# An attention kernel without its closing barrier, with its first two projection chunks interleaved and its last product cut unevenly

## The chip, the cores and the metric

The kernel runs on one core of a Trainium2 chip. A core has five engines, each with its own instruction stream: TensorE (PE in the profile, with its weight loads shown apart as PEld), VectorE (DVE), ScalarE (ACT), GpSimd (POOL) and SyncE (SP, which here issues every DMA). [...] The metric is device time in microseconds (us).

## The reference

Eight sequences of 112 queries are projected, attend to cached keys and values with 32 heads, and are projected back. All inputs and the output are bf16.

```python
B, Sq, D = 8, 112, 640
H, Sk, Dh = 32, 512, 192
q = transpose((x @ wq).reshape(B, Sq, H, Dh), 0, 2, 1, 3)
scores = einsum("bhqd,bhkd->bhqk", q, k_cache) * Dh ** -0.5
p = softmax(scores, axis=-1)
o = einsum("bhqk,bhkd->bhqd", p, v_cache)
return transpose(o, 0, 2, 1, 3).reshape(B, Sq, H * Dh) @ wo
```

The caches are 50 MB each and are read once.

## The kernel before

**Units.** `build_main` handles heads in `NG = 8` groups of four. A unit is one group of heads of one sequence, so there are `NU = 64` units. For each unit PE computes the scores (`do_S`, L925), ACT takes the exponential of them (L1023), PE multiplies by the values (`do_PV`, L943; a column of ones beside the values gives the row sums), DVE and ACT divide by those sums (`do_NM`: the reciprocal L1089 and the scaling L1092 on DVE; `norm` L1030 on ACT), PE transposes the result (`do_T`, L954), and ACT copies it into `oT` (L1040).

**Projections.** For each group, six chunks of 128 query columns are projected (`("Q", g, c)`), and after the attention of a group seven row tiles of 128 rows go through its part of `wo` (`("O", g, m)`), whose partial products DVE adds up in `acc` (`do_OE`, L1101 and L1104). Both kinds are called pairs, since each has two halves that go to PSUM banks 6 and 7. A table written out by hand (`slot`, filled by `put` and `halves`) gives each iteration `i` up to two of them: slot `(i, 0)` stands between the transposes and the product with the values, slot `(i, 1)` after that product. Before a pair writes a bank, `bank_free` waits until the pair before it has been copied out: for an O pair this is the semaphore `vO`, which DVE raises in `do_OE`.

**The start.** The first group is projected in two halves of the rows (`do_Q0`). For the first half of the rows, chunks 0 to 3 read `wq` as it landed, with four narrow matmuls (32 columns of weights each, L871) for each of the `DC = 5` blocks of the contraction; chunks 4 and 5 read a copy that POOL has reordered (L864). Chunk 0 waits for each of the five loads of `wq` (`mW0`) as it comes to it. Even chunks go to bank 6, odd ones to bank 7, and a chunk waits until ACT has copied out the chunk two before it (`aQ`).

**Keys.** Each unit's keys come as four loads into one of three buffers `kr`, and DVE transposes them in four instructions (`do_KT`, L1083) into `kt`. `kt_ahead` says how many of them DVE has done by each iteration; from iteration 17 on it is always the transposes 1, 2 and 3 of one unit and transpose 0 of the next. SP issues the loads in one fixed order (L1284). A load of keys waits until the fourth transpose of the unit that had its buffer is done (`vKT`), and everything behind it in SP's order waits with it.

**DVE's order in an iteration** (L1127 to L1138): up to three key transposes (`kts[:3]`), then the evacuation of the O pair in slot `(i, 0)`, then the reciprocal and scaling of unit `i - 1`, then the O pair in slot `(i, 1)`, then the remaining transposes.

**The end.** The last O pair (`apart` in `do_pair`) finishes one half of 320 columns before it starts the other. For each of the seven row tiles SP sends the 128 x 640 result to HBM when both halves have been added (L1287), and at last waits for all seven (L1290).

**Fallback and blocks.** POOL counts row sums outside a safe range; the count reaches every engine as a register (`get_flag`). `br_eq` (L1306) then sends the engines past a second, slower kernel that is only there for a count above zero, and that isn't entered here. The work of each engine is written inside one `nc.Block()` (L834; its closing instructions carry L757 in the profile). Such a block makes each engine branch into instructions of its own at the start, and at the end each engine branches out and takes part in a barrier of all five; only after it comes `br_eq`.

Of the kernel before, what the change touches and what calls it, by code (L numbers as in the profile page):

```python
# [666 lines left out]
def build_main(nc, x, k_cache, v_cache, wq, wo, out, flag, regs, hints):  # L667
    B, SQ, D = x.shape
# [7 lines left out]
    HQ = R // 2  # L676
    HO = D // 2
    scale = float(DH) ** -0.5
    LO, HI = 2.0 ** -30, 2.0 ** 40
# [77 lines left out]
    with ExitStack() as es:  # L757
# [3 lines left out]
        def sem(name):  # L761
            return es.enter_context(nc.semaphore(name))
# [48 lines left out]
        mWO = [[sem(f"mWO{j}{c}") for c in range(3)] for j in range(2)]  # L811
        mOUT = [sem(f"mOUT{j}") for j in range(MT)]
        XM = [(0, 2), (2, 4), (4, MT)]
# [19 lines left out]

        block = es.enter_context(nc.Block())  # L834

        @block.tensor
        def _(pe):
            def do_X(m):
# [8 lines left out]
            def held(out, lhsT, rhs, start, stop):  # L847
# [4 lines left out]
                    ldweights=False))  # L852

            def do_Q0(c, h):
                n = q_index[0, c, h]
                if c == 0:
                    W(pe, vX, 3 if h == 0 else 4)
                    W(pe, aX, 2 if h == 0 else 4)
                W(pe, aQ, n - 1)
                for dc in range(DC):  # L860
                    if h == 1 or c >= RAW:
                        if h == 0 and c == RAW:
                            W(pe, gW0, dc + 1)
                        mm = pe.matmul(ps[:, 6 + n % 2, 0:HQ], wq0[:, dc, 128 * c:128 * (c + 1)], xT[:, dc, HQ * h:HQ * (h + 1)],  # L864
                                       start=(dc == 0), stop=(dc == DC - 1))
                        continue
                    if c == 0:
                        W(pe, mW0[dc], 16)
                    for a in range(4):
                        w0 = DH * a + 64 * (c // 2) + c % 2  # L870
                        mm = pe.matmul(ps[32 * a:32 * a + 32, 6 + n % 2, 0:HQ], wqs[:, 0, dc, w0:w0 + 63:2],  # L871
                                       xT[:, dc, HQ * h:HQ * (h + 1)], start=(dc == 0), stop=(dc == DC - 1))
                mm.then_inc(pQ, 1)

            def do_pair(i, j):
# [15 lines left out]
                for q, hs in [(q, [h]) for h in range(2) for q in steps] if apart else [(q, range(2)) for q in steps]:  # L891
                    if k == "Q":
                        w = wqs[:, g % 2, q, 128 * c:128 * (c + 1)]
                        rhs = [xT[:, q, HQ * h:HQ * (h + 1)] for h in range(2)]
                    else:
                        if c == 0 and q % 2 == 0:
                            W(pe, mWO[g % 2][q // 2], 32 * (g // 2 + 1))
                        w = oT[:, q, 128 * c:128 * (c + 1)]
                        rhs = [wos[:, g % 2, q, HO * h:HO * (h + 1)] for h in range(2)]
                    for h in hs:  # L900
# [3 lines left out]
                        for f in range(cuts):  # L904
                            cs = slice(width * f // cuts, width * (f + 1) // cuts)
                            mm = (pe.matmul if h == hs[0] and f == 0 else held)(ps[:, 6 + h, cs], w, rhs[h][:, cs], q == 0,  # L906
                                                                               q == n - 1 and f == cuts - 1)
# [57 lines left out]
            for j in range(BRIDGE):  # L965
                (held if j else pe.matmul)(ps[:, 7, 0:128], wt[:], wt[:], True, True)
            for c in range(6):
                do_Q0(c, 0)
# [22 lines left out]

        @block.scalar
        def _(act):
            W(act, vI, 1)
# [75 lines left out]

        @block.vector
        def _(dve):
            dve.memset(wt[:], 0.0).then_inc(vW, 1)
# [21 lines left out]
            def do_OE(g, m, h):  # L1095
                n = o_index[g, m, h]
                W(dve, pO, n + 1)
                src = ps[:, 6 + h, 0:HO]
                cs = slice(HO * h, HO * (h + 1))
                if g == 0:  # L1100
                    ins = dve.tensor_copy(acc[:, m, cs], src)  # L1101
# [46 lines left out]

        @block.gpsimd
        def _(gp):  # L1150
            gp.memset(ident[:], 0.0).then_inc(gI0, 1)
# [58 lines left out]

        @block.sync
        def _(sp):
            loads = []
# [65 lines left out]
            for n, (dst, src, s, count, waits) in enumerate(loads):  # L1279
# [4 lines left out]
                sp.dma_start(dst, src).then_inc(s, 16)  # L1284
            for m in range(MT):
                W(sp, vO, 2 * (MT * (NG - 1) + m + 1))
                sp.dma_start(out.rearrange("b s d -> (b s) d")[128 * m:128 * (m + 1)], ob[:, m, :]).then_inc(mOUT[m], 16)  # L1287
            get_flag(sp)
            for m in range(MT):
                sp.wait_ge(mOUT[m], 16)  # L1290


def bass_standalone__mha_block_cached__near_ridge_kernel(
# [8 lines left out]
    with nc.sbuf_tensor("flag", [1, 1], I32) as flag:  # L1302
        regs, hints = {e: nc.alloc_register(e, "raised") for e in mybir.ALL_ENGINES}, {}
        build_main(nc, x, k_cache, v_cache, wq, wo, out, flag, regs, hints)
        for e, loc in hints.items():
            nc.engines[e].br_eq(regs[e], 0, on_true="main_end", on_false="main_again").branch_hint(loc)  # L1306
# [33 lines left out]
```

## Time and profile before

| what | value |
|---|---|
| five runs | 397.04, 399.2, 396.1, 397.09, 396.75 us; median 397.04 us |
| profiled execution | 397.61 us, of which the span (first to last instruction of the kernel) is 395.8 us; 1.8 us lie around it |
| granted TensorE clock | 1.00 of full speed over the span |
| PE matmul busy | 387.4 us, 98% of the span, 8865 matmuls |
| DVE, ACT, POOL busy | 283.7 us (72%), 251.0 us (63%), 152.9 us (39%) |
| DMA | 120.00 MB, mean 303 GB/s; the hardware queue's packets take 90.4% of the 16 engines' span |

The page gives for each engine its busy time, and in 40 equal slices of the span its busy share in tenths (9 is 90% or more). The chain of waits follows the work that ended last back to the start; each of its lines is a start, a length and what ran. A timeline line is a start, a length, the engine, the source line, the operation, output and inputs with shapes, a count, and in brackets the idle time before it and what ended that. A line of the waits view says who waited for whom, and then the total in us, how often, and the longest. A source view gives for each kind of instruction of one line its count, its durations in ns as min/median/max, and its first and last start. A `q` behind an engine's name means its instruction queue.

### The profile page before, as it was taken

The numbers are of one execution on the slowest core, as the hardware profiler recorded it, in microseconds if no ns is written. First come the engines' busy times: TensorE is split into PE (matmuls) and PEld (weight loads), VectorE is DVE, ScalarE is ACT, GpSimd is POOL, SyncE is SP. The second block draws the span as 40 slices with busy tenths as digits, with TensorE's granted clock in tenths as the row PEclk, the third lists the DMA queues.
The fourth block names the chain that finished last, engine by engine and source line by source line (L and its number), as shares of the span: only waits on it lengthen the run. The fifth ranks groups of instructions, "written<-read, shape, count | busy, mean of one in ns | idle before, by whom it ended". The sixth has DMA issues, their size and how long they took to land.

```text
span 395.8 us, 19841 instructions
## 1 busy us (share of the span) xinstructions
PE 387.4 (98%) x8865; PEld 242.4 (61%) x8262; DVE 283.7 (72%) x506; ACT 251.0 (63%) x550; POOL 152.9 (39%) x352
## 2 busy tenths in 40 slices
PE   7999999999999999999999999999999999999995
PEld 2555666666566666656566566666566666667672
DVE  1665678687786777776687676877588677789833
ACT  3767765766656765666755767566674766667661
POOL 5523444334343345235343255324354233234420
PEclk9999999999999999999999999999999999999999
DMA  8999999999999999989999999989998799989811
GB/s 274 375 369 364 329 290 359 360 340 305 354 341 331 336 289 371 313 270 312 331 311 324 295 324 322 336 275 311 308 316 276 225 301 304 349 260 305 268 39 65
DMA packets 88440, 120.00 MB, mean 303 GB/s; under 512 B 9760, under 2 KB 88352, under 8 KB 88352
## 3 DMA queue, kind: packets, MB, share of 16 engines
q1 hardware_dynamic: 88352, 118.72, 90.4%
q8 instruction: 68, 1.11, 1.2%
q14 instruction: 20, 0.16, 0.1%
HBM read 117.54 MB, written 1.15 MB: 300 GB/s over the span
## 4 chain that ended last, share of the span: by engine, by line
PE 93%; DMA 3%; DVE 2%; issue 1%; SPq 1%; DVEq 0%
PE ps L943 22%; PE ps L906 21%; PE ps L848 21%; PE ps L925 21%; PE ps L954 6%; PE ps L864 2%; DMA kr<-in_k_cache_dram 1%; DMA wqs<-in_wq_dram 1%; DVE kt L1083 1%; PE ps L871 1%; SPq L1284 1%; DVE xs L1104 0%; PE ps L844 0%; DVE acc L1104 0%; DVE rinv L1089 0%
## 5 line engine op out<-in xcount | busy, mean ns | idle before, releaser
L1083 DVE STREAM_TRANSPOSE kt<-kr 128x384 int32<-128x384 int32 x256 | 192.5, 873 | 8.7 <-DMA kr<-in_k_cache_dram 8.6
L1023 ACT ACTIVATE pT<-ps 128x448 bf16<-128x448 f32 x256 | 130.6, 559 | 84.3 <-PE ps L925 84.0
L925 PEld LDWEIGHTS ps<-qT,kt 32*128 32x128 bf16 x6144 | 77.3, 93 | 31.7 <-issue 23.4
L906 PE MATMUL ps<-wos,oT 128*128 128x320 bf16 x342 | 93.0, 298 | 1.0 <-DVE xs L1104 0.7
L943 PE MATMUL ps<-vm,pT 128*128 128x193 bf16 x768 | 91.5, 247 | 0.2
L848 PE MATMUL ps<-wos,oT 128*128 128x320 bf16 (+1 forms) x340 | 91.3, 296 | 0.1
L925 PE MATMUL ps<-qT,kt 32*128 32x112 bf16 x6144 | 88.2, 208 | 1.5 <-issue 1.3
L1200 POOL TENSOR_SCALAR bad<-rinv 112x4 f32<-112x4 f32 x64 | 14.6, 228 | 192.8 <-DVE rinv L1089 192.7
L1183 POOL COPY vm<-vs 128x1152 int32<-128x1152 int32 x64 | 73.4, 1147 | 23.5 <-issue 15.0
L943 PEld LDWEIGHTS ps<-vm,pT 128*128 128x128 bf16 x768 | 67.8, 97 | 21.2 <-ACT oT L1040 11.1
L848 PE MATMUL ps<-xT,wqs 128*128 128x448 bf16 (+2 forms) x226 | 74.1, 341 | 0.0
L906 PE MATMUL ps<-xT,wqs 128*128 128x448 bf16 (+1 forms) x210 | 73.5, 350 | 0.0
L1030 ACT ACTIVATE os<-ps,rinv 112x192 bf16<-112x192 f32 x128 | 47.9, 436 | 28.3 <-DVE rinv L1089 28.3
L943 PE MATMUL ps<-vs,pT 128*128 128x193 bf16 x256 | 62.6, 245 | 0.0
L906 PEld LDWEIGHTS ps<-wos,oT 128*128 128x128 bf16 x342 | 33.2, 97 | 44.5 <-issue 37.0
L1007 ACT ACTIVATE qT<-ps 128x448 bf16<-128x448 f32 x96 | 48.0, 552 | 19.3 <-PE ps L906 12.4
L1089 DVE RECIPROCAL rinv<-ps 112x4 f32<-112x4 f32 x64 | 11.6, 182 | 58.3 <-PE ps L943 58.3
L1104 DVE TENSOR_TENSOR acc<-ps,acc 128x320 f32<-128x320 f32 x84 | 37.2, 485 | 20.7 <-PE ps L906 20.7
L1040 ACT ACTIVATE oT<-ps 128x672 bf16<-128x672 bf16 x64 | 46.4, 725 | 2.1 <-PE ps L954 2.1
L906 PEld LDWEIGHTS ps<-xT,wqs 128*128 128x128 bf16 x210 | 20.4, 97 | 34.2 <-issue 29.4
L1092 DVE TENSOR_TENSOR os<-ps,rinv 112x384 bf16<-112x384 f32 x64 | 35.7, 558 | 6.9 <-DVE rinv L1089 0.5
L1176 POOL COPY wqs<-wqr 128x384 bf16<-128x384 bf16 x70 | 33.3, 508 | 4.0 <-DMA wqr<-in_wq_dram 3.9
(42 smaller groups left out, 154.8 us busy)
## 6 DMA issues: line engine op xcount, KB each, us to landing
kr<-in_k_cache_dram SPq DMA_DIRECT2D x256, 192.0 KB, 4.1
vs<-in_v_cache_dram SPq DMA_DIRECT2D x256, 192.0 KB, 4.0
wos<-in_wo_dram SPq DMA_DIRECT2D x48, 160.0 KB, 4.2
wqr<-in_wq_dram SPq DMA_DIRECT2D x35, 192.0 KB, 5.4
out_dram<-xs SPq DMA_DIRECT2D x7, 160.0 KB, 1.8
wqs<-in_wq_dram SPq DMA_DIRECT2D x5, 192.0 KB, 4.4
xs<-in_x_dram SPq DMA_DIRECT2D x2, 320.0 KB, 3.4
xs<-in_x_dram SPq DMA_DIRECT2D x1, 480.0 KB, 5.5
```

Of the source, the lines that this page charges most:

```text
L848: return pe.add_instruction(mybir.InstMatmult(name=nc.get_next_instruction_name(), engine=mybir.EngineType.PE, ins=[pe.lower_ap_or_imm(rhs ...
L906: mm = (pe.matmul if h == hs[0] and f == 0 else held)(ps[:, 6 + h, cs], w, rhs[h][:, cs], q == 0, q == n - 1 and f == cuts - 1)
L925: mm = pe.matmul(ps[:, a, SQ * t:SQ * (t + 1)], kt[u % NT][p, t, c // 2, :, c % 2], qT[g % 2][p, c, SQ * b:SQ * (b + 1)], start=(c == 0), ...
L943: mm = pe.matmul(pv[:, k, e, 0:DH + 1], pT[u % 2][:, a, t, :], src[:, a, v0:v0 + DH + 1], start=(t == 0), stop=(t == 3), skip_group_check= ...
L1007: act.activation(qT[g % 2][:, c, HQ * h:HQ * (h + 1)], ps[:, 6 + (n % 2 if g == 0 else h), 0:HQ], ACTF.Copy).then_inc(aQ, 1)
L1023: act.activation(pT[u % 2][:, a, :, 0:SQ], ps[:, a, 0:4 * SQ].rearrange("p (t q) -> p t q", t=4), ACTF.Exp, scale=scale).then_inc(aEX, 1)
L1030: ins = act.activation(os_[u % 2][:, DH * (2 + e):DH * (3 + e)], pv_of(u)[0:SQ, 1, e, 0:DH], ACTF.Copy, scale=rinv[:, u % 4, 2 + e:3 + e])
L1040: act.activation(oT[:, :, SQ * b:SQ * (b + 1)].rearrange("p (k c) q -> p k c q", k=2), src.rearrange("p k (c q) -> p k c q", c=3), ACTF.Co ...
L1083: dve.transpose(dst, src).then_inc(vKT, 1)
L1092: dve.tensor_tensor(os_[u % 2][:, 0:2 * DH].rearrange("p (e d) -> p e d", e=2), pv[0:SQ, 0, :, 0:DH], rinv[:, u % 4, 0:2][:, :, None].broa ...
L1104: ins = dve.tensor_tensor(ob[:, m, cs] if g == NG - 1 else acc[:, m, cs], src, acc[:, m, cs], op=ALU.add)
L1183: gp.tensor_copy(vm[u % NM][:].rearrange("p a (t w) -> p a t w", w=RW)[:, :, :, 0:DH].bitcast(I32), vs[u % NV][:, :, 32:32 + 3 * DH].rearr ...
```

## The change

Five edits are made.

1. The five engine programs become plain functions that are called one after the other in the main program, so there is no block. The barrier moves into the fallback, which begins with one.
2. `do_Q0_first` replaces `do_Q0` for chunks 0 and 1 of the first half of the rows. It goes over the five contraction blocks outermost: it waits for one load of `wq`, and does the four matmuls of chunk 0 and the four of chunk 1 for it. Its matmuls are the same 40 in another order. It waits for the loads only, and chunks 2 to 5 follow as before.
3. The last O pair is cut into 384 and 256 columns (`HL`), on PE and in DVE's additions.
4. The last row tile is sent in two DMAs, the first when its first half is added.
5. On DVE, the third key transpose of an iteration moves behind the evacuation of the O pair in slot `(i, 0)`, and so stands between it and the reciprocal of unit `i - 1`. In iterations without an O pair there, nothing moves.

```diff
+    HL = 384
...
-        mOUT = [sem(f"mOUT{j}") for j in range(MT)]
+        mOUT = [sem(f"mOUT{j}") for j in range(MT + 1)]
...
-        block = es.enter_context(nc.Block())
-
-        @block.tensor
-        def _(pe):
+        def on_tensor(pe):
...
+            def do_Q0_first():
+                W(pe, vX, 3)
+                W(pe, aX, 2)
+                for dc in range(DC):
+                    W(pe, mW0[dc], 16)
+                    for c in range(2):
+                        for a in range(4):
+                            w0 = DH * a + 64 * (c // 2) + c % 2
+                            mm = pe.matmul(ps[32 * a:32 * a + 32, 6 + c, 0:HQ], wqs[:, 0, dc, w0:w0 + 63:2],
+                                           xT[:, dc, 0:HQ], start=(dc == 0), stop=(dc == DC - 1))
+                        if dc == DC - 1:
+                            mm.then_inc(pQ, 1)
...
-                        rhs = [wos[:, g % 2, q, HO * h:HO * (h + 1)] for h in range(2)]
+                        rhs = [wos[:, g % 2, q, HL * h:HL + (D - HL) * h] if apart else wos[:, g % 2, q, HO * h:HO * (h + 1)]
+                               for h in range(2)]
...
-                            cs = slice(width * f // cuts, width * (f + 1) // cuts)
+                            cs = slice(0, (HL, D - HL)[h]) if apart else slice(width * f // cuts, width * (f + 1) // cuts)
...
-            for c in range(6):
+            do_Q0_first()
+            for c in range(2, 6):
                 do_Q0(c, 0)
...
-                src = ps[:, 6 + h, 0:HO]
                 cs = slice(HO * h, HO * (h + 1))
+                if (g, m) == (NG - 1, MT - 1):
+                    cs = slice(HL * h, HL + (D - HL) * h)
+                src = ps[:, 6 + h, 0:cs.stop - cs.start]
...
-                for it in kts[:3]:
+                for it in kts[:2]:
                     do_KT(*it)
                 if i < NU:
                     do_OEs(i, 0)
+                for it in kts[2:3]:
+                    do_KT(*it)
                 if i >= 1:
                     do_NM(i - 1)
...
-            for m in range(MT):
-                W(sp, vO, 2 * (MT * (NG - 1) + m + 1))
-                sp.dma_start(out.rearrange("b s d -> (b s) d")[128 * m:128 * (m + 1)], ob[:, m, :]).then_inc(mOUT[m], 16)
+            parts = [(m, 0, D) for m in range(MT - 1)] + [(MT - 1, 0, HL), (MT - 1, HL, D)]
+            for n, (m, d0, d1) in enumerate(parts):
+                W(sp, vO, 2 * (MT * (NG - 1) + m + 1) - (d1 == HL))
+                sp.dma_start(out.rearrange("b s d -> (b s) d")[128 * m:128 * (m + 1), d0:d1], ob[:, m, d0:d1]).then_inc(mOUT[n], 16)
             get_flag(sp)
-            for m in range(MT):
-                sp.wait_ge(mOUT[m], 16)
+            for n in range(len(parts)):
+                sp.wait_ge(mOUT[n], 16)
+
+        for part, eng in ((on_tensor, nc.tensor), (on_scalar, nc.scalar), (on_vector, nc.vector), (on_gpsimd, nc.gpsimd), (on_sync, nc.sync)):
+            part(eng)
...
         with nc.body("main_again"):
+            nc.all_engine_barrier()
             build_mha_kernel(nc, x, k_cache, v_cache, wq, wo, out)
```

More of the change, by code (lines that the diff above doesn't have):

```diff
@@ L856, in do_Q0 @@
                 if c == 0:
-                    W(pe, vX, 3 if h == 0 else 4)
-                    W(pe, aX, 2 if h == 0 else 4)
+                    W(pe, vX, 4)
+                    W(pe, aX, 4)
                 W(pe, aQ, n - 1)
@@ L866, in do_Q0 @@
                         continue
-                    if c == 0:
-                        W(pe, mW0[dc], 16)
                     for a in range(4):
@@ L990, in _, with on_scalar @@
             get_flag(pe)
-        @block.scalar
-        def _(act):
+        def on_scalar(act):
             W(act, vI, 1)
@@ L1069, in _, with on_vector @@
             get_flag(act)
-        @block.vector
-        def _(dve):
+        def on_vector(dve):
             dve.memset(wt[:], 0.0).then_inc(vW, 1)
@@ L1147, in _, with on_gpsimd @@
             get_flag(dve)
-        @block.gpsimd
-        def _(gp):
+        def on_gpsimd(gp):
             gp.memset(ident[:], 0.0).then_inc(gI0, 1)
@@ L1209, in _, with on_sync @@
             get_flag(gp)
-        @block.sync
-        def _(sp):
+        def on_sync(sp):
             loads = []
```

## The prediction

> **What bounds the kernel now.** I read the page first, then the chain of waits in order of time, then the timeline at the places where that chain leaves PE, and last the source views of the closing lines.
>
> ```profile
> span 395.8 us, 19841 instructions
> PE 387.4 (98%) x8865; PEld 242.4 (61%) x8262; DVE 283.7 (72%) x506; ACT 251.0 (63%) x550; POOL 152.9 (39%) x352
> PE   7999999999999999999999999999999999999995
> ...
> DMA  8999999999999999989999999989998799989811
> ```
>
> PE is busy in every slice but the first and the last. A change inside the span therefore gains only where PE stands still, at the start, at the end, or at one of the few gaps between, and the chain of waits names these:
>
> ```profile
> 3.67 4.50 DMA wqs<-in_wq_dram
> 8.21 3.21 PE ps L871 x64
> ...
> 96.99 2.35 DVE kt L1083 x3
> 99.36 5.88 DMA kr<-in_k_cache_dram
> ...
> 106.69 0.85 DVE kt L1083
> 107.53 0.73 DVE acc L1104 x2
> ...
> 392.24 0.49 DVE xs L1104
> ```
>
> The chain starts with the last load of `wq`, which PE awaits until 8.21. Around 107 us it goes through DVE, in the only stretch of the interior where another engine's work is on it for long. It leaves PE at 392.24 for the last addition. The timeline at the first two places:
>
> ```profile
> 8.64 0.54 ACT L1007 ACTIVATE qT<-ps 128x448 bf16<-128x448 f32 x1 [2.60 <-PE ps L871]
> 9.58 0.54 ACT L1007 ACTIVATE qT<-ps 128x448 bf16<-128x448 f32 x1 [0.40 <-PE ps L871]
> ...
> 105.26 2.27 DVE L1083 STREAM_TRANSPOSE kt<-kr 128x384 int32<-128x384 int32 x3 [0.22 <-DMA kr<-in_k_cache_dram]
> 107.39 0.86 DVE L1104 TENSOR_TENSOR acc<-ps,acc 128x320 f32<-128x320 f32 x2
> 107.91 0.31 PE L906 MATMUL ps<-wos,oT 128*128 128x320 bf16 x1 [0.36 <-DVE acc L1104]
> 108.30 0.30 PE L848 MATMUL ps<-wos,oT 128*128 128x320 bf16 x1
> ```
>
> At the end, the source views of the closing lines:
>
> ```profile
> L1290 SPq EVENT_SEMAPHORE  x3: 28/28/28, 393.7 to 394.6; - x3
> L757 SPq COMPARE_BRANCH  x1: 78/78/78, 394.6 to 394.6; - x1
> L757 SPq DRAIN  x1: 7/7/7, 395.0 to 395.0; - x1
> L757 SPq EVENT_SEMAPHORE  x1: 17/17/17, 395.2 to 395.2; - x1
> L1306 SPq COMPARE_BRANCH  x1: 65/65/65, 395.3 to 395.3; - x1
> L1306 PEldq COMPARE_BRANCH  x1: 485/485/485, 395.3 to 395.3; - x1
> ```
>
> SP has seen the last output land at 394.6. Everything after it, up to 395.8, is the way out: SP's branch, the barrier, and the five branches of L1306, PE's being the longest.
>
> **The change part by part.** The sum is made against the profiled execution, 397.61 us (395.8 of span and 1.8 around it), which lies 0.57 above the median of the five runs, 397.04. I take the saving off the median.
>
> *Closing barrier.* SP's output wait ends at 394.6 and a branch of 65 to 78 ns follows it, after which SP is out; so the span would end at 394.7 in place of 395.8, a saving of 1.1. PE, ACT, POOL and DVE have their registers before 392.9 and branch out while SP still waits, so PE's 485 ns is covered by the output DMA. If SP's own branch should cost what PE's does, 0.4 of it comes back: 0.7 at least. Upward, the four engines may also do early some of what lies in the 1.8 us around the span; no row divides these, so 1.1 to 2.0. I take 1.1, the row itself.
>
> [...]
>
> *Opening branch.* SP's first DMA issue starts at 0.74, and the trace's records have its release from the opening barrier end at 0.68. The branch between is worth 0 to 0.06; I take 0.03.
>
> *First two chunks.* The loads come some 0.5 us apart (PE restarts at 6.73, 7.23, 7.69, 8.21), and four narrow matmuls start every 0.19 (3.21 us over 16 such fours with their tail), so eight fit between two loads. After 8.21 PE has 12 fours left of L871 and not 16, which would be 0.75. But chunk 2 needs bank 6, and ACT's copy of chunk 0 still runs 8.64 to 9.18, since chunk 0 still ends with the last load. PE then waits from about 8.6 to 9.24 (0.055 us is what PE takes to follow a semaphore elsewhere in this trace). Chunk 2 started at 9.36 before. The gain is 0.12; chunk 1's copy ends at 9.72, before chunk 3 needs it at 10.2. POOL's copies, which chunk 4 needs, end at 10.39, and chunk 4 moves to about 11.25. Some of it can be lost to ACT's copies later: 0 to 0.12, taken as 0.1.
>
> *Third key transpose behind the O evacuation.* At 105.26 three transposes run 0.71 apart, and only then the additions that PE awaits, though the products were done at 106.1 and 106.2. With two ahead, the additions start at 106.68 and not 107.39. Their first `vO` comes at 107.14; PE is ready for it at 107.39, the end of the product with the values. The second comes at 107.53, where PE wants it at 107.53. Two gaps go, 0.52 and 0.25 as starts stand against the usual spacing; with some 0.1 left, 0.6 is gained. Without the 0.22 us wait for keys it would still be 0.55, so it isn't an accident of one late load. The bounds are 0 (an execution where the keys come earlier) and 0.77. What is late next is the transpose itself. Who waits for it:
>
> ```profile
> SPq L1284 <- DVE kt L1083: 40.6, 89, 1.7
> ...
> DVE acc L1104 <- PE ps L906: 20.7, 28, 1.4
> DVE acc L1101 <- PE ps L906: 5.2, 5, 1.3
> ```
>
> SP queues key loads behind it, and behind these the loads of values and weights. In the iterations where DVE now idles up to 1.4 us ahead of the evacuation, the transpose comes up to 1.4 + 0.9 + 0.6 = 2.9 us later. Once it has run, the reciprocal waits for it too: at 42.50 to 43.98 DVE adds for 0.89 and idles 0.59 before the reciprocal, and a transpose of 0.72 pushes it by 0.15. PE needs that result about 1.0 us after it is ready in nearly all units (the starts of L954 against the ends of L1030 and L1092), so this push costs nothing. For the loads: DVE waits for keys 8.6 us in all, 8.1 of them in two waits before 22 us, and key transposes are some two units ahead of PE. I take nothing for it, and keep the loss as a rival.
>
> *Last product and last DMA.* PE's 12 matmuls have the same columns in all. The first half ends 0.16 later and the second at the same time, near 392.2. The last addition shrinks from 320 to 256 columns: with 482 ns for 320 and 558 ns for the 384 of L1092, about 0.41, so 0.08 earlier. The first DMA (SP issue 0.33) starts near 392.2, so SP is free for the second at 392.65. That one carries 64 KB in place of 160, and a 160 KB output lands 1.8 us after its issue, whose packets fill the last 0.5 or so. So 0.05 to 0.35; taken 0.15.
>
> [...]
>
> Sum: 1.1 + 0.03 + 0.1 + 0.6 + 0.15 = 1.98. The profiled execution would go to 395.6 and the median to **395.0 us**, 0.5% less. A measurement of this kernel can tell about 0.5% (2 us) from no change, which puts the bound at 395.05, right at the forecast.
>
> **The rivals.**
>
> *Less is had.* The gap at 107 us closes differently in other executions, or part of the barrier's 1.1 comes back after the span. Without the 0.6 the time is 395.6; with only 0.7 at the end as well, 396.0. For it: the DMA slices stand at 9, so loads in that stretch land when the queue lets them. Against: 0.55 of the gap does not need the late load.
>
> *More is had outside the span.* Four engines leave 1 to 3 us before SP. If half of the 1.8 us around the span can be done by them meanwhile, 0.9 more is gained: 394.1. For it: after the span the trace still has instruction fetches, at 396.3 to 397.8. Against: SP's own share stays.
>
> *Slower: key loads starve.* The later transpose frees a key buffer late, SP's order stands still, and with DMA at 9 tenths the lost load time can't be made up. At worst each of some 12 iterations where DVE waited over a microsecond for the O product costs one transpose of 0.72 on PE's path: 8.6 lost against 1.4 gained elsewhere, 404.2. It decides once five of them do: 3.6 - 1.4 is 2.2 us more than before. For it: SP already awaits DVE 89 times. Against: DVE waits for keys four times in all.
>
> *The change doesn't do what it says* holds for the first chunks alone: 0.1 and not 0.75 is that rival's price, already taken.
>
> **How the numbers follow.** The forecast's case has 50%, with a range of its own from 394.5 to 395.5, a little over half of it below 395.05. Less is had: 24%, within 0.5%. More: 20%, faster. Slower: 6%. So faster 0.48, same 0.46, slower 0.06. PE also stops inside its scores for up to 0.7 us at a few places that the profile calls issue (33.6 and 281.6 us), 2.4 us over the span with the smaller ones; these may fall otherwise, by 0.7 either way. The range reaches from 393.9 (the case with more, and a little beyond) to 396.6 (the smallest terms with such stops added).
>
> **What would show it.** The closing: no L757 rows, SP's branch of L1306 within 0.2 us of its last output wait, and PE's some 2 us ahead of it. The first chunks: PE idle near 0.6 us before chunk 2, and the first scores at 14.1 where they stood at 14.19. The order: no wait of L906 on DVE near 107, and PE ahead by 0.7 from there on. The end: two output DMAs for the last tile, about 0.5 us apart. The prediction is wrong if PE's busy share falls in the interior, if DVE's waits for key loads grow beyond 10 us, or if the time around the span grows by what the span loses.

## The result, and the profile after

The changed kernel took 397.14 us (median of 36 runs, 395.53 to 400.73) beside 397.68 us for the kernel before, measured with it (62 runs). The ratio is 0.9989, with a 95% interval of 0.9976 to 1.0003: by the ratio 0.44 us less (the medians differ by 0.54), and not told apart from no change. The prediction was 395.0, 1.98 us below the 397.04 it started from.

The profiled execution took 396.12 us, 394.4 of them span. First the head of the page:

```profile
span 394.4 us, 19831 instructions
PE 386.6 (98%) x8865; PEld 243.0 (62%) x8262; DVE 284.2 (72%) x506; ACT 250.8 (64%) x550; POOL 152.7 (39%) x352
```

By the span alone 1.4 us seem to be won, but nearly all of that is luck. The places that the edits touch give 0.71 at 107 us and 0.07 in the last product, and lose 0.32 at the start and 0.36 at the end: together 0.1 us. The rest comes mostly where PE stood still in the execution before at two of the stops that the prediction names (33.6 and 281.6 us), which don't come in this one. The waits view puts PE's waits ahead of scores that the profile calls issue at 1.3 us before and at 0.3 here. Single executions of one kernel differ by a microsecond and more, so what follows is read locally.

The timeline of PE at the start (L860 are the first two chunks, L880 chunks 2 and 3, L875 chunks 4 and 5):

```profile
8.09 1.12 PE L860 MATMUL ps<-xT,wqs 128*32 128x448 bf16 x20
9.67 2.08 PE L880 MATMUL ps<-xT,wqs 128*32 128x448 bf16 x40 [0.46 <-ACT qT L1017]
11.68 0.55 PE L875 MATMUL ps<-xT,oT 128*128 128x448 bf16 x2
```

PE idles 0.46 us ahead of chunk 2, for ACT's copy of chunk 0, as predicted (near 0.6 was expected). But nothing is gained here: the first scores start at 14.52, where 14.1 was predicted and 14.19 stood before. The experiments come back to that. Around 107 us, DVE and then PE:

```profile
105.28 1.58 DVE L1092 STREAM_TRANSPOSE kt<-kr 128x384 int32<-128x384 int32 x2 [0.19 <-DMA kr<-in_k_cache_dram]
106.70 0.87 DVE L1115 TENSOR_TENSOR acc<-ps,acc 128x320 f32<-128x320 f32 x2
107.50 0.83 DVE L1092 STREAM_TRANSPOSE kt<-kr 128x384 int32<-128x384 int32 x1
107.30 0.30 PE L916 MATMUL ps<-wos,oT 128*128 128x320 bf16 x1
107.62 0.30 PE L846 MATMUL ps<-wos,oT 128*128 128x320 bf16 x1
```

The additions start at 106.70 and PE has no bracket with DVE any more. Of the two gaps, 0.52 and 0.25 us over the usual spacing, 0.19 is left.

The end, from the chain of waits and the source views of the closing lines (L1302 SP's waits for the outputs, L1321 the branches):

```profile
388.68 1.80 PE ps L916 x12
390.50 0.42 DVE xs L1115
```

```profile
L1302 SPq EVENT_SEMAPHORE  x4: 17/28/28, 391.9 to 394.2; - x4
L1321 ACTq COMPARE_BRANCH  x1: 68/68/68, 389.5 to 389.5; - x1
L1321 PEldq COMPARE_BRANCH  x1: 1005/1005/1005, 389.6 to 389.6; - x1
L1321 POOLq COMPARE_BRANCH  x1: 65/65/65, 389.6 to 389.6; - x1
L1321 DVEq COMPARE_BRANCH  x1: 84/84/84, 391.1 to 391.1; - x1
L1321 SPq COMPARE_BRANCH  x1: 70/70/70, 394.3 to 394.3; - x1
```

No barrier is left, and SP branches 0.07 us after its last wait, as predicted. But that wait ends at 394.2, and the last addition at 390.93. Before, 1.82 us lay between the two (392.74 and 394.56); now it is 3.3. From the last addition to the end of the span it was 3.08 us before, and is 3.44 now. In this execution the closing has become longer, with the barrier removed and the last DMA cut.

The view of the DMA between 391.0 and 395.5, in 40 slices of 0.11 us (busy share of the 16 engines in tenths, then GB/s), shows what happened:

```profile
DMA  0039840599020000001001000000000000000030
GB/s 0 0 109 300 280 130 0 155 282 251 5 73 0 0 0 0 0 7 14 7 7 14 11 23 9 0 0 0 0 0 0 0 0 0 0 0 0 0 73 0
q1 hardware_dynamic: 288, 0.16, 12.4%
q14 instruction: 2, 0.02, 1.4%
q8 instruction: 1, 0.02, 1.3%
```

The two humps are the two output DMAs. Both are over by 392.2 on most engines. Then comes a pause, and from 392.9 to 393.8 a trickle of 7 to 23 GB/s. The packet records say what it is: 8 rows of the first DMA and then 8 rows of the second, a sixteenth of the 128 rows of each, which is taken for the share of one of the 16 DMA engines, since each DMA has 16 landings in the records (9,776 for 611). They account for the pause too: the q8 line is one packet of 16 KB, of the kind that the records call instruction, from 392.02 to 392.98, and the late rows start at its end, from 392.96 on. It is taken for a fetch of PE's instructions by its count: queue 8 has 69 of them in this profile, the other four engines have some 2,650 instructions together, and PE has 17,180. The records name a packet's queue and not its DMA engine, so that the fetch and the late rows share an engine is inferred from this order. Of the first DMA's 16 shares 15 had landed by 392.06 and the last at 394.06; of the second's, 15 by 392.50 and the last at 394.22. The same view of the profile before, from 392.7 to 395.5, has one hump and no instruction queue:

```profile
DMA  0000000000002789999510000000000000000000
q1 hardware_dynamic: 144, 0.16, 16.4%
```

There all five engines branched out after the barrier, and their fetches came at 396.3 to 397.8, behind the span; the prediction had even cited them, as a rival's evidence.

### The profile page after: what moved, and what is told of

It reads as the page before. It is cut to its first block, busy times and chain, and to the rows that moved or that the text cites. A ratio compares the mean times of both kernels' runs of the same rounds, so it can differ in the third digit from the quotient of the medians.

```text
span 394.4 us, 19831 instructions
## 1 busy us (share of the span) xinstructions
PE 386.6 (98%) x8865; PEld 243.0 (62%) x8262; DVE 284.2 (72%) x506; ACT 250.8 (64%) x550; POOL 152.7 (39%) x352
## 2 busy tenths in 40 slices
DMA packets 88588, 120.04 MB, mean 304 GB/s; under 512 B 9776, under 2 KB 88496, under 8 KB 88496
## 3 DMA queue, kind: packets, MB, share of 16 engines
q8 instruction: 69, 1.13, 1.2%
## 4 chain that ended last, share of the span: by engine, by line
PE 93%; issue 2%; SPq 2%; DVE 1%; DMA 1%; POOL 0%; ACT 0%; ACTq 0%
PE ps L953 22%; PE ps L846 21%; PE ps L916 21%; PE ps L935 20%; PE ps L964 6%; SPq L1295 2%; DMA xs<-in_x_dram 1%; PE ps L842 1%; DVE kt L1092 1%; PE ps L880 1%; PE ps L875 1%; PE ps L860 0%; DVE xs L1115 0%; DMA vs<-in_v_cache_dram 0%; POOL vm L1195 0%
## 5 line engine op out<-in xcount | busy, mean ns | idle before, releaser
L1092 DVE STREAM_TRANSPOSE kt<-kr 128x384 int32<-128x384 int32 x256 | 196.2, 872 | 9.9 <-DMA kr<-in_k_cache_dram 9.8
L916 PE MATMUL ps<-wos,oT 128*128 128x320 bf16 (+2 forms) x342 | 93.0, 298 | 0.7 <-DVE xs L1115 0.7
L935 PE MATMUL ps<-qT,kt 32*128 32x112 bf16 x6144 | 87.3, 208 | 0.9 <-ACT pT L1033 0.6
L953 PEld LDWEIGHTS ps<-vm,pT 128*128 128x128 bf16 x768 | 67.8, 97 | 21.2 <-ACT oT L1050 11.1
L1098 DVE RECIPROCAL rinv<-ps 112x4 f32<-112x4 f32 x64 | 11.1, 174 | 46.4 <-PE ps L953 46.4
```

What stands on the lines that cost most here:

```text
L935: mm = pe.matmul(ps[:, a, SQ * t:SQ * (t + 1)], kt[u % NT][p, t, c // 2, :, c % 2], qT[g % 2][p, c, SQ * b:SQ * (b + 1)], start=(c == 0), ...
L953: mm = pe.matmul(pv[:, k, e, 0:DH + 1], pT[u % 2][:, a, t, :], src[:, a, v0:v0 + DH + 1], start=(t == 0), stop=(t == 3), skip_group_check= ...
L1092: dve.transpose(dst, src).then_inc(vKT, 1)
```

## The experiments

The theory after this comparison: an engine that branches out fetches instructions 1.1 to 2.5 us later (PE's branch started at 395.33 and its fetch at 396.56 before, 389.6 and 392.02 after), through one of the DMA engines that carry the output, and what that engine still has to send of the output waits. The barrier had kept those fetches behind the last output (394.56 before, the first of them at 396.3); without it they meet it. Rivals: the narrow rows of the two last DMAs (768 and 512 bytes) are slow in themselves, or the late share was an accident of one execution. The local measure is the time from the end of the last addition to the last landing, and to the end of the span; it is free of what happens in the interior.

**The changed kernel again**, unedited.

> The changed kernel once more. Its first profile had the last addition end at 390.93, the last output landed at 394.23 and the span ended at 394.37, so 3.4 us from the last addition to the end (before: 392.74, 394.58 and 395.82, 3.1 us). Fetch theory (without the barrier PE branches out early, its 16 KB of instructions are fetched by one of the DMA engines that carry the last output, and that engine's share lands 1.7 us late): again 3.2 to 3.5 us from the last addition to the last landing, with 15 of 16 shares landed some 1.7 us before the last. Split theory (two DMAs with rows of 768 and 512 bytes are slow): the same sum, but on more engines than one. Accident theory: about 1.8 us this time. Time against before: about 0.5 us less by the first two theories, 1.5 to 2 less by the third.

Measured: 397.06 us beside 397.05, ratio 1.0004 (0.9987 to 1.0021). 2.93 us to the last landing, less than the 3.2 to 3.5 expected, and 3.08 to the end. The lateness came again but in another form. SP's issue of the last DMA, on the timeline:

```profile
392.01 1.71 SPq L1299 DMA_DIRECT2D out_dram<-xs  x1
```

An issue of the last DMA took 0.35 us in the other profile. This one started inside PE's fetch (391.89 to 393.34) and ended 0.38 after it, so the whole second DMA was late and landed at 394.74 to 394.92. Of the first DMA's shares the last landed 1.06 after the other 15 (2.0 in the other profile). The same happens all through the kernel, where nobody notices: in the profile of before 64 of SP's 610 issues take over 0.6 us, 52 of these end 0.28 to 0.40 after the end of a PE fetch, and of the 546 short ones a single one does.

**PE held to the last addition.** The only edit is a wait, on an engine that has nothing left to do:

```diff
             get_flag(pe)
+            W(pe, vO, 2 * MT * NG)
```

> The changed kernel, and PE waits for the last addition before it branches out; nothing else differs, and PE has nothing to do in that time. Fetch theory: PE's fetch starts about 1.4 us later (it came 2.45 us after PE's branch started), behind most of the last output, which then lands 1.8 to 2.0 us after the last addition; the span is about 1.4 us shorter than that of the changed kernel, and the time 1.0 to 1.5 us below it, 1.5 to 2.0 below before. If the fetch comes only 1.2 us after the branch, as it did in the profile of before, it still meets the last packets and half of that is lost. Split theory: landing 3.3 us after the last addition as in the changed kernel, no gain in time.

Measured: 395.69 us beside 397.05, ratio 0.9976 (0.9954 to 0.9999). 1.58 us to the last landing, less than the 1.8 to 2.0 expected, and 1.74 to the end. PE's fetch came at 395.20, and the last output landed at 395.05 to 395.23. The two narrow DMAs are unchanged here, so their rows are not slow in themselves. The fetches of ACT and POOL still ran early, at 393.29 to 393.91, beside the first of the two DMAs, and delayed nothing.

**One last DMA.**

```diff
-            parts = [(m, 0, D) for m in range(MT - 1)] + [(MT - 1, 0, HL), (MT - 1, HL, D)]
+            parts = [(m, 0, D) for m in range(MT)]
```

> The changed kernel with its last row tile sent in one DMA, as before, and all else as in the changed kernel. Split theory: the landing is back at 1.8 us after the last addition, and the time falls by 1.4 us. Fetch theory: PE still branches out early, one DMA engine is still held by its fetch for about 1 us, and the last landing is 2.5 to 3.5 us after the last addition with 15 of 16 shares at 1.8 us; the time stays within 0.4 us of the changed kernel's.

Measured: 395.70 us, ratio 0.9975 (0.9956 to 0.9994). 2.10 us to the last landing, 2.26 to the end. PE's fetch ran from 393.62 to 394.70, ahead of most of the packets of a DMA issued at 393.78, and so only one share was late, by 0.24. The 2.10 are below what the fetch theory gave: it had 2.5 to 3.5 us here. The author's reading is that what a fetch costs hangs on what it meets, and that here the DMA met less of it; the run shows the order and the 0.24. The kernel's time missed the fetch theory too: 1.4 us below the changed kernel's, which is what the split theory had, and not within 0.4 of it. But PE held and the barrier back, which keep the split, came out 1.4 and 1.3 below as well, so these times don't tell the three apart; the landings do, and they speak against the split theory. Without any lateness the single DMA lands 1.80 us after its issue (before, and in two later profiles), and the second of two 1.53 after its own: the split is worth some 0.3, if it is left alone.

**The barrier back.**

```diff
             part(eng)
+        nc.all_engine_barrier()
```

> The changed kernel with a barrier of all five engines put back ahead of the branches, and still no block. Fetch theory: no instructions are fetched before the last landing, which is 1.8 us after the last addition or a little earlier; then the barrier and the branches take 0.7 to 1.2 us, so 2.5 to 3.0 us from the last addition to the end of the span, and the time is 0.4 to 0.9 us below the changed kernel's although it has one barrier more. Split theory: the landing stays at 3.3 us and the barrier comes on top, 4.0 to 4.5 us, and the time is 0.7 to 1.2 us above the changed kernel's.

Measured: 395.80 us, ratio 0.9982 (0.9965 to 0.9998). All 16 shares landed within 0.18 us of one another, 1.56 after the last addition; the end came at 2.46. So with a barrier *more* this closing is 0.4 to 1.0 us shorter than that of the changed kernel. From the last landing to the end the barrier costs 0.90, where a kernel without it has 0.15: this barrier itself is worth 0.75 us. Before it was 1.26 from the last landing to the end: there the block's way out comes ahead of the barrier, with SP's branch at 394.64 and its drain at 395.0.

**The barrier removed, and nothing else.** The first edit of the five, alone on the kernel before.

```diff
-        block = es.enter_context(nc.Block())
...
+        for part, eng in ((on_tensor, nc.tensor), (on_scalar, nc.scalar), (on_vector, nc.vector), (on_gpsimd, nc.gpsimd), (on_sync, nc.sync)):
+            part(eng)
```

> The kernel before with one edit alone: no block and no barrier on the normal path. The prediction gave this edit 1.1 us. Fetch theory: PE leaves about 1.4 us ahead of the last addition, as in the run with one last DMA, and its fetch meets the output; from the last addition to the end of the span 2.2 to 3.4 us in place of 3.08, so a gain of 0 to 0.9 and a time 0 to 0.9 us below before. If the prediction's step was right: 2.0 us, and 1.1 below before. The interior is that of before: PE waits about 0.36 us for DVE at 107 us.

Measured: 396.76 us beside 397.91, ratio 0.9968 (0.9946 to 0.999). 2.21 us to the last landing, where 1.82 is usual, and 2.36 to the end. PE's fetch ran from 392.69 to 393.77, and DVE's 8 KB from 394.15 to 394.75; one share landed 0.35 after the other 15. So 0.72 of the edit's 1.1 is had locally in this one profile; the measured time, 1.27 less by the ratio (0.4 to 2.1), is too wide to tell 0.7 from 1.1. With its last DMA whole and later, the edit alone does better at the closing than the five together.

**PE held longer.** This was to move PE's fetch safely behind the output:

```diff
             get_flag(pe)
+            pe.wait_ge(mOUT[MT - 1], 16)
```

> The changed kernel, with PE waiting until the first DMA of the last row tile has landed (about 1.0 us after the last addition) before it branches out. Holding it to the last addition put its fetch at 395.20 while the last output landed at 395.05 to 395.23, so the next fetch could still meet it; here the branch (0.49 us) lies beside the second DMA's landing and the fetch, 1.2 to 2.5 us after the branch, behind it. Fetch theory: last landing 1.55 to 1.6 us after the last addition, end of the span 1.7 to 1.8 after it, and a time as with PE held to the last addition or 0.1 to 0.4 below it, 1.3 to 1.8 below before. A theory in which holding PE helped by chance: about the time of before again.

Measured: 396.76 us beside 397.91, ratio 0.9963 (0.9941 to 0.9985). But 3.01 us to the last landing and 3.16 to the end, so the local expectation failed, and with it the theory in its first form. PE's fetch came at 395.00, behind everything. The late share follows another fetch: 8 KB, by the timing for DVE, which had branched at 392.09, were fetched from 393.28 to 393.94, and the last 8 rows of the second DMA start right behind it, from 393.94 on; 15 shares had landed by 393.80, the 16th did at 394.93. SP's issue took 0.65 us, until 0.3 after an 8 KB fetch that ended at 392.29. So by this order a fetch of 8 KB can do it as well (1.13 us late here), though not each one does: two of them, from 393.29 to 393.91, delayed nothing where PE was held to the last addition.

**All four held.** The wait for the first of the last two DMAs, on PE, ACT, DVE and POOL. It ends 1.14 us after the last addition, so that the branches (0.49 us for PE) lie beside the second DMA's landing.

```diff
             get_flag(pe)
+            pe.wait_ge(mOUT[MT - 1], 16)
...
             get_flag(act)
+            act.wait_ge(mOUT[MT - 1], 16)
...
             get_flag(dve)
+            dve.wait_ge(mOUT[MT - 1], 16)
...
             get_flag(gp)
+            gp.wait_ge(mOUT[MT - 1], 16)
```

> The changed kernel, with PE, ACT, DVE and POOL all waiting until the first DMA of the last row tile has landed before they branch out; SP goes as before. In the run with PE alone held so, 8 packets of the last DMA ran only at 394.0, right behind an 8 KB fetch at 393.28 to 393.94, 1.2 us after DVE's branch, and SP's issue of that DMA took 0.65 us, until 0.3 us after POOL's fetch. Theory as widened (the exit fetch of any engine holds one DMA engine, and an issue of SP): no fetch between the first output DMA of the last tile and the last landing, the last DMA's issue takes 0.33 to 0.36, it lands 1.55 to 1.6 us after the last addition on all 16 engines, the span ends 1.7 to 1.8 after it (before: 3.08, changed: 3.08 and 3.44), and the time is 1.2 to 1.7 us below the changed kernel's and 1.6 to 2.1 below before. If only PE's fetch matters, the late share comes again, and 2.5 to 3.0 us from the last addition to the end.

Measured: 396.52 us beside 397.61, ratio 0.9968 (0.9939 to 0.9996). 1.56 us to the last landing, 1.71 to the end, and no fetch until 0.6 us after the span's end. The closing is as expected to 0.05 us. The time is above the expectation: 1.27 below before by the ratio (0.2 to 2.4), where 1.6 to 2.1 was expected, and by the medians 0.46 below the changed kernel beside it, where 1.2 to 1.7 was. The profiled execution itself was long (397.6 of span): PE stopped for 1.96 us at 34.35, of which below, and by the trace's clock records it then had half the clock from 37.46 to 40.88: its matmuls of 448 columns start 0.37 us apart from 37.51 on, and 0.19 just ahead of that.

**All four held, first chunks as before.** The first two chunks' edit is undone on top.

```diff
-            do_Q0_first()
-            for c in range(2, 6):
+            for c in range(6):
                 do_Q0(c, 0)
```

> The kernel of the run with all four engines held, with the first two chunks as before the change. If the interleaved chunks gain 0.1 us, as the prediction has it, this one is 0.1 slower; from the profiles so far (scores of the second unit at 21.5 to 21.8 us with the old chunks in three profiles, 21.5 to 22.5 with the interleaved ones in seven) it is 0 to 0.3 faster. The closing is the same, 1.7 to 1.8 us from the last addition to the end; 1.7 to 2.2 below before in all.

> The kernel with four engines held and the old first chunks once more, since its time was known to 1 us only (1.4 below before, interval 0.4 to 2.3). Sum of the local terms: 1.37 at the end (1.71 in place of 3.08 us from the last addition on), 0.5 to 0.9 at 107 us and 0.07 in the last product: 1.9 to 2.3 below before, with 1.71 us again from the last addition to the end and no fetch in that time. If part of that is lost elsewhere, 1.0 to 1.5 again; the fetch stops of PE near 27 and 34 us are then the first place to look.

Measured: 396.17 us beside 397.61, ratio 0.9965 (0.9941 to 0.9989), and in the second set 395.42 beside 397.98, ratio 0.9929 (0.9902 to 0.9956). Weighted by their intervals the two give 0.9949 (0.9931 to 0.9967), 2.0 us less (1.3 to 2.7). By its ratio the first is 1.4 below before, less than the 1.7 to 2.2 expected, and the second 2.8, more than the 1.9 to 2.3. 1.71 us from the last addition to the end both times. The second profile, with the same view of the DMA from 391.0 to 395.5 and the closing lines (L1294 SP's waits, L1313 the branches):

```profile
DMA  0000029940594000000000590020000000000000
GB/s 0 0 0 0 0 89 314 314 151 7 164 287 128 5 0 0 0 0 0 0 0 0 146 218 0 0 73 0 0 0 0 0 0 0 0 0 0 0 0 0
```

```profile
L1294 SPq EVENT_SEMAPHORE  x4: 17/28/28, 392.2 to 392.9; - x4
L1313 ACTq COMPARE_BRANCH  x1: 68/68/68, 392.4 to 392.4; - x1
L1313 PEldq COMPARE_BRANCH  x1: 490/490/490, 392.5 to 392.5; - x1
L1313 SPq COMPARE_BRANCH  x1: 70/70/70, 392.9 to 392.9; - x1
```

The two humps have no tail, and the fetches stand by themselves at the right, beyond the span's end at 393.0. PE's 0.49 us is over when SP leaves. This version is faster than the kernel before, by more than the noise.

**The changed kernel twice more**, each beside a held one.

> The changed kernel a third time, beside the two with the engines held. Fetch theory: again one share of the last output late or its issue held, 2.3 us or more from the last addition to the end, with a fetch seen at that time; its time 1.2 to 1.7 above the runs with all engines held, and 0 to 0.8 below before. Accident theory: 1.75 us from the last addition to the end, and the same time as with the engines held.

> The changed kernel beside it. Fetch theory: 2.3 to 3.5 us from the last addition to the end, its time 0.7 to 1.7 above the held one and 0 to 0.8 below before. If holding the engines is worth nothing in time: equal to the held one.

Measured: 396.98 beside 397.61, ratio 0.9978 (0.9956 to 1.0), and 397.20 beside 397.98, ratio 0.9970 (0.9951 to 0.999). From the last addition to the end 2.92 and 2.83 us, with PE's fetch at 392.06 and 393.60 and one share of both last DMAs late each time by 0.9 to 1.25 us. The held version with the old first chunks, beside them, took 0.8 and 1.8 us less; the first of these differences is not clear of the scatter by itself. With the first two profiles the closing is 3.44, 3.08, 2.92 and 2.83, on average 3.07, and before it was 3.08: no accident, and what the barrier and the cut DMA gave is gone on average. Weighted by their intervals, the four ratios of the changed kernel give 0.9988 (0.9979 to 0.9996), 0.5 us less than before.

**DVE's order alone, and the first chunks alone**, each on the kernel before, one execution each (398.17 and 397.11 us, which alone say nothing).

```diff
-                for it in kts[:3]:
+                for it in kts[:2]:
                     do_KT(*it)
                 if i < NU:
                     do_OEs(i, 0)
+                for it in kts[2:3]:
+                    do_KT(*it)
```

> The kernel before with one edit alone: DVE's third key transpose behind the evacuation of the O pair. By the prediction: the waits of PE's O products for DVE near 107 us (0.52 and 0.25 over the usual spacing) go down to 0.2 or less, so PE's work from 108 us on lies 0.6 earlier against its work at 104 us than before; no new wait of PE on DVE or on loads; the closing stays at 3.1 us from the last addition to the end. Rival (key loads starve): DVE's waits for keys grow from 8.6 us to over 10 and PE gets waits elsewhere. One execution's time differs by 1 us and more from the next, so only the local numbers are read.

```diff
-            for c in range(6):
+            do_Q0_first()
+            for c in range(2, 6):
                 do_Q0(c, 0)
```

> The kernel before with one edit alone: the first two chunks with the contraction outermost. By the prediction: PE idles 0.45 to 0.6 us ahead of chunk 2, until ACT has copied chunk 0, and the chunks 4 and 5 start about 0.1 earlier against the landing of the last load of wq than before. If the edit gave all that it moves, chunk 2 would start 0.75 earlier and the idle time would not be there. If all loads have landed before PE comes to them, nothing is gained and the idle time of about 0.45 is a loss, as in the profile of the changed kernel, where the chunks 4 and 5 started 0.3 later than before.

*DVE's order.* The time from the scores that begin near 102.7 us to those of the next unit, against the shortest of all profiles (6.30): with the old order 0.90, 0.53 and 0.50 us more (before, barrier alone, first chunks alone), with the new order 0.19 once and 0.00 in eleven profiles, this one's included. DVE's waits for keys are between 7.4 and 11.8 us with the new order, and were 8.6, 10.8 and 8.0 with the old. So they passed the 10 us that the prediction named as a sign in two profiles with the new order (11.1 and 11.8) and in one with the old. PE's weight loads wait a little longer for transposes, 3.4 to 3.9 us in all where it was 1.7 to 3.2, and no gap of PE's matmuls comes from it. The old order in the profile of the first chunks alone, on DVE and PE:

```profile
104.37 3.67 DVE L1097 STREAM_TRANSPOSE kt<-kr 128x384 int32<-128x384 int32 x5
107.88 0.88 DVE L1118 TENSOR_TENSOR acc<-ps,acc 128x320 f32<-128x320 f32 x2
```

```profile
108.42 0.31 PE L919 MATMUL ps<-wos,oT 128*128 128x320 bf16 x1
108.81 0.30 PE L848 MATMUL ps<-wos,oT 128*128 128x320 bf16 x1
```

Five transposes stand ahead of the additions, and the second O product starts 0.39 after the first, where 0.14 is usual.

*The first chunks*, with the last load of `wq` awaited (first profile below, first chunks alone) and with each load there before PE comes to it (second, all four held):

```profile
6.27 1.84 PE L862 MATMUL ps<-xT,wqs 128*32 128x448 bf16 x32
8.85 0.56 PE L862 MATMUL ps<-xT,wqs 128*32 128x448 bf16 x8 [0.75 <-DMA wqs<-in_wq_dram]
9.88 2.08 PE L884 MATMUL ps<-xT,wqs 128*32 128x448 bf16 x40 [0.46 <-ACT qT L1021]
11.89 0.55 PE L877 MATMUL ps<-xT,oT 128*128 128x448 bf16 x2
```

```profile
7.17 2.08 PE L860 MATMUL ps<-xT,wqs 128*32 128x448 bf16 x40
9.71 2.08 PE L880 MATMUL ps<-xT,wqs 128*32 128x448 bf16 x40 [0.45 <-ACT qT L1018]
11.72 0.55 PE L875 MATMUL ps<-xT,oT 128*128 128x448 bf16 x2
```

In both PE idles 0.45 us ahead of chunk 2. In the first, chunk 4 starts 3.08 us after the last load has landed (8.81). With the old chunks that stretch is 3.18 to 3.19 in all five profiles, also where PE began as late as 6.94 and 7.07. So 0.11 is gained, where PE waits for the loads. In the second PE began at 7.17 and waited for no load, and the idle time is on its path: chunk 4 starts 4.55 after that, and 3.60 after the last load, a loss of 0.41. Of the ten profiles with interleaved chunks five show 3.07 to 3.08, the other five 3.16 to 3.60; on average it is 3.23, a loss of 0.04. Which it is goes with the start of TensorE's clock records. The trace has them begin, with the full clock, at 4.2 to 5.2 us in the five with the gain, and PE begins its chunks at 6.02 to 6.35; in the other five they begin at 5.4 to 6.8, and PE begins at 6.67 to 7.17. Ahead of them PE's transposes of `x`, matmuls of 128 columns, go at half the pace: in the profile after, whose records begin at 6.81, they start 0.107 us apart until 6.4, and in the profile before, whose records begin at 4.22, 0.055 from 4.24 on.

## Why the prediction was wrong

**The step that failed** is the closing barrier, 1.1 us: "PE, ACT, POOL and DVE have their registers before 392.9 and branch out while SP still waits, so PE's 485 ns is covered by the output DMA." Its branch is covered: in the profile after it is over by 390.6. What follows the branch is not: the fetch of instructions, from 392.02 to 392.98, falls on the output DMA that is meant to cover it, whose last share landed at 394.22, 1.7 us behind the other 15. The term was bounded at 0.7 to 2.0, and its upper bound came from work that the four engines might do early; that this early work could hold up SP's last wait was not among the bounds, nor was it a rival. Alone the edit gave 0.72 locally in the one profile of it, at its lower bound and not for the reason given for that bound. Together with the last DMA cut in two, it gives 0 on average: 3.07 us from the last addition to the end, where 3.08 stood. With the four engines held it is 1.71.

**Last product and last DMA**, 0.15: the product's part is right (from the start of the last unit's scores to the end of the last addition it is 13.51 us and was 13.58: 0.07, predicted 0.08). The second DMA's part is 0.27 with all four held (1.55 us to the last landing in place of 1.82), so the term would be 0.34, at the upper end of 0.05 to 0.35; in the changed kernel this part went the way of the barrier's. Where nothing held them up, the 64 KB landed 1.53 us after their issue and the 160 KB 1.80.

**Third key transpose**, 0.6: right, 0.5 to 0.9 in three profiles with the old order; the 0.9 lies above its upper bound of 0.77. **Opening branch**, 0.03: SP's first issue stands at 0.74 in both profiles, so nothing. **First two chunks**, 0.1: right in its mechanism and its size where PE waits for the loads, and mis-sized as a term, since its lower bound of 0 left out the executions in which PE comes late and loses up to 0.41; on average -0.04.

So what came is 0.64 at 107 us (the mean of the three) and 0.07, less 0.04 at the start, together 0.67; 0.5 (0.2 to 0.8) was measured over the four sets. With all four engines held and the old chunks it is 1.37 for the closing, 0.64 and 0.07: 2.08, against 2.0 (1.3 to 2.7) measured. The prediction's sum of 1.98 (which taken off 397.04 gives 395.06, written as 395.0) was about what the edits could give, and the closing is where it went.

**The rivals.** "More is had outside the span" fell: the time around the span is 1.81 to 1.92 us before, as medians, and 1.75 to 1.84 in the changed kernel and most of its variants; with all four engines held it is 1.83 to 2.02, up to 0.2 above the kernel before beside it. In the changed kernel nothing of the barrier's cost was seen to come back there. "Key loads starve" fell: no gap of PE's matmuls came of it, though the waits for keys passed 10 us in two profiles. "Less is had" came nearest, by another way than it said: the loss came inside the span, ahead of SP's last wait. The median of 397.14 lies above the range's 396.6, partly because the kernel before read 397.68 in that set and not 397.04. Against its own kernel before, 0.44 less is as far as the range went (397.04 to 396.6), and it went so far only by adding stops of PE to the smallest terms; these terms alone, 0.7 and 0.05, come to 0.75.

## What to carry to other kernels

In this kernel the barrier at the end also kept the engines' exit fetches behind the last output (396.3 against 394.56), so removing it was only half an edit. What worked was to hold each idle engine on a semaphore that comes late enough for its fetch to fall behind the last landing, and early enough that its branch is over when the last engine leaves: 1.71 us from the last addition to the end, where 3.07 on average stood without it. What was hidden here used what covered it: a fetch of 16 KB fell on the output DMA, and a share of the output landed 0.9 to 2 us late in the four profiles of the changed kernel. So "hidden behind the DMA" is to be checked for DMA work, instruction fetches among it. Where executions scatter by a microsecond, a closing is best judged from a fixed event (here the last addition) to the end of the span, which was 1.71 us in all three profiles with the four engines held, where no fetch falls into it.

## What the hardware showed that was not expected

- The fetches of instructions are packets of 16 KB for PE (0.9 to 1.7 us at the end) and of 8 KB for the others (0.3 to 0.7 us). In seven of the eight profiles without a barrier in which engines were let go early, a sixteenth of an output came 0.2 to 2 us late behind such a fetch. Most issues of SP that start inside a PE fetch (39 of 45 in the profile before) take over 0.6 us, and of the 64 issues there that take so long 52 end 0.28 to 0.40 us after a PE fetch (at the closing 0.33 us grew to up to 1.71).
- PE's own stops named issue lie behind its fetches. At the stop near 34 us PE goes on with the same matmul in eleven profiles, 1.37 to 1.53 us after a fetch has ended (before, it ended at 32.69 us and PE went on at 34.12; with PE held, at 34.96 and 36.49). In the profile after, a fetch ended earlier, at 31.85, and PE has no stop there. That PE waits there for a fetch that comes late is the author's reading. These stops vary more than the 0.7 us that the prediction allowed: near 34 us they are under 0.2 in four of fifteen profiles, 0.3 to 1.1 in seven, and 1.5 to 2.2 in four. They are the largest single part of the scatter that was found. What sets them was not tried.
- In the profiles before and after, PE has 69 fetches of 16 KB for some 17,180 instructions, 249 to one; the packets taken for the other engines' fetches are of 8 KB. If the reading above holds, one near 34 us cost PE up to 2.2 us.
- TensorE's clock records begin at 4.0 to 6.8 us in thirteen of the fifteen profiles (the other two have none), and PE's transposes start 0.107 us apart ahead of that and 0.055 behind it. When the first projection begins, and whether the interleaved chunks gain or lose, goes with it.
